# Seven block products instead of eight in the up projection of the last four feed-forward units

## The chip, the cores and the metric

One core of one Trainium2 chip. The metric is the device time of one execution, in microseconds, as the median of several runs. The profile of the kernel before is one execution taken by the hardware profiler; in it L416 means line 416 of the kernel before.

## The reference

Two layers with shared weights, each a long convolution over 2048 positions with 512 channels, and then a gated feed-forward network with 1792 features:

```python
def _A_ref(q, k, v, shift_k, ssm_k, ssm_D):
    ...                                   # k_shift: causal convolution of k with 4 taps
    kv = k_shift * v
    ...                                   # y: causal convolution of kv with ssm_k (length 2048), by FFT
    y = y + kv * ssm_D[None, None, :]
    return q * y

def _B_ref(x, w_gate, w_up, w_down):
    g = _silu(x @ w_gate)                 # x: 2048 x 512, w_gate and w_up: 512 x 1792
    u = x @ w_up
    return (g * u) @ w_down               # w_down: 1792 x 512

x = A_q
x = x + _A_ref(_layernorm(x, axis=-1), A_k, A_v, A_shift_k, A_ssm_k, A_ssm_D)
x = x + _B_ref(_layernorm(x, axis=-1), B_w_gate, B_w_up, B_w_down)
x = x + _A_ref(_layernorm(x, axis=-1), A_k, A_v, A_shift_k, A_ssm_k, A_ssm_D)
x = x + _B_ref(_layernorm(x, axis=-1), B_w_gate, B_w_up, B_w_down)
return x
```

All inputs and the output are bfloat16.

## The kernel before

The 2048 positions are cut into four blocks (c = 0 to 3) of 512. The convolution is computed once, as products of block spectra (tiles X, G, Z), because k, v and the filter are the same in both layers; its result for a block is the tile Yk. A **unit** (layer, c, h) is 256 positions of one layer: half h of block c. There are 16 units. The order of the program text is, for each c: (0,c,0), (0,c,1), (1,c,0), (1,c,1), with the convolution of later blocks between. So the last four units are (0,3,0), (0,3,1), (1,3,0), (1,3,1), and (1,3,0) needs the result of (0,3,0), as (1,3,1) needs that of (0,3,1).

**Before a unit** (`prologue`): mean and variance of the rows of x (L914, L915 on VectorE, the power -1/2 on GpSimd at L905), the normalised rows n, the product with Yk (L986) and the sum into x (L987), then the second norm, whose result z (L964) is transposed by a DMA that SyncE issues (L994) into zT: 128 channels by 4 channel blocks by 2 row sets by 128 rows.

**A unit** (`ffn`) goes through the 14 feature tiles of 128 features in groups of 4, 4, 4 and 2 (`GROUPS`). For a group there are two forms:

- *Column-wise* (from L1169): the weights are stationary and zT moves, so that features come out on the partitions and 256 positions in the columns. Matmuls of 256 columns write a PSUM tile pf (L416, the helper `mm`), two feature tiles in one bank. ScalarE copies gate values through Silu into sg (L1183) and up values into ht (L1187), and VectorE multiplies them (L1190).
- *Row-wise* (`by_rows`): zT is stationary and 512 weight columns move (also L416). ScalarE evacuates to sg and hr (L1123, L1124), VectorE multiplies (L1127, L1130), and a DMA transpose issued by SyncE (L1132) turns the product back into sg.

`ROWWISE` says how many of a unit's groups, from the first, take the row-wise form: 2 in (0,3,0), 1 in (0,3,1), 2 in (1,3,0), 0 in (1,3,1). For the down product of some groups (`STRASSEN`: all four groups in (0,3,0), (0,3,1) and (1,3,0), the first two in (1,3,1)) the kernel already uses seven block products instead of eight: sums of weight blocks made once by `weight_sums` (L1049), sums of activations cb (L1064, L1066, L1068 on VectorE), matmuls of 256 columns (L1085), four PSUM banks evacuated by ScalarE into mt (L1097) and combined into x by VectorE (L1102 to L1109). Other groups use the plain down product into pd (L1210).

**Order.** All operations are first put into a plan with the buffers that they read and write. Buffers are taken from rings of fixed size; "pf" has 4 PSUM banks, "s8" 11 slots of SBUF, "ht" 7. The table `ORDER` gives each operation of the plan its place in one overall sequence, and so fixes the order of instructions on each engine. It holds 1716 places.

Of the kernel before, what the change touches and what calls it, by code (L numbers as in the profile page):

```python
# [9 lines left out]
P = 128  # L10
F32 = mybir.dt.float32
# [3 lines left out]
ALU = mybir.AluOpType  # L15
# [13 lines left out]
ROWWISE = lambda l, c, h: 0 if (l, c, h) == (0, 0, 0) else {(0, 3, 0): 2, (0, 3, 1): 1, (1, 3, 0): 2, (1, 3, 1): 0}[l, c, h] if c == 3 else 3 if l == 1 else 2  # L29
ROWSPLIT = lambda l, c, h: 3 if c == 3 else 2  # L30
STRASSEN={(1,2,1):4,(0,3,0):4,(0,3,1):4,(1,3,0):4,(1,3,1):2}
I_RING = lambda k: "pf" if k == 3 else "pc"
# [311 lines left out]
def kernel(  # L344
# [175 lines left out]
    def dve(n, fn, r, w, one=False, cost=None, **kw):  # L520
        add("DVE", cost or (tt1(n) if one else tt2(n)), fn, r=r, w=w, **kw)
# [1007 lines left out]
```

## Time and profile before

| | |
|---|---|
| median of 3 runs | 339.26 us (339.04 to 339.29) |
| span of the profiled execution | 337.7 us (the page gives no other time of it) |
| instructions | 5898 |
| TensorE matmuls | 330.9 us busy, 2141 recorded |
| VectorE | 299.9 us busy |
| ScalarE | 262.8 us busy |
| GpSimd | 35.4 us busy |

The span runs from the first to the last instruction of that execution. Ends of matmuls are modelled, so the spacing of their starts says more than their durations. Groups of instructions are named by line, engine, operation, and the tiles written and read (out<-in); the number behind x counts them. A timeline row gives start, length, engine, line, operation, tiles, shape and count of a stretch of like instructions.

### The profile page before, as it was taken

How to read it: one execution, taken by the hardware profiler on the slowest of the kernel's cores; microseconds unless marked ns; L12 is line 12 of the kernel's file. 1: busy time of each engine (PE TensorE's matmuls, PEld its weight loads, DVE VectorE, ACT ScalarE, POOL GpSimd, SP SyncE). 2: the span in 40 equal slices, each digit the busy share in tenths (PEclk: the TensorE clock that was granted, in tenths of full speed). 3: DMA queues.
4: the chain of work that ended last, by engine and by line, in shares of the span. 5: the costliest groups of instructions: out<-in, count | busy, mean ns of one | idle time of the engine just before them, and what ended most of it. 6: DMA issues, size and time to landing. Idle time of an engine off the chain costs nothing.

```text
span 337.7 us, 5898 instructions
## 1 busy us (share of the span) xinstructions
PE 330.9 (98%) x2141; PEld 204.6 (61%) x2172; DVE 299.9 (89%) x512; ACT 262.8 (78%) x534; POOL 35.4 (10%) x48
## 2 busy tenths in 40 slices
PE   9999999999999999999999999999999999999996
PEld 7655864645445564745454464744455687858884
DVE  8899999999888998999999999999999787877545
ACT  7889999999967466999899894999675556475462
POOL 4050001102100000122010100011100100100000
PEclk9999999999999999999999999999999999999999
DMA  7999604632346147421324434510514230204101
GB/s 255 350 229 376 130 13 66 151 82 41 71 93 94 36 91 188 95 49 32 62 53 106 97 60 110 138 35 16 96 28 82 56 72 17 48 18 93 49 3 62
DMA packets 77993, 31.59 MB, mean 94 GB/s; under 512 B 69766, under 2 KB 75787, under 8 KB 77963
## 3 DMA queue, kind: packets, MB, share of 16 engines
q1 hardware_dynamic: 77808, 31.13, 39.6%
q8 instruction: 17, 0.28, 0.4%
q14 instruction: 14, 0.11, 0.1%
q10 hardware_dynamic: 154, 0.07, 0.1%
HBM read 12.33 MB, written 2.10 MB: 43 GB/s over the span
## 4 chain that ended last, share of the span: by engine, by line
PE 91%; ACT 4%; DMA 2%; issue 1%; DVE 1%; SPq 1%
PE pf L416 56%; PE pd L1210 20%; PE ps L1085 7%; PE ps L416 6%; DMA kTb<-in_A_k_dram 1%; PE wm L1495 1%; DMA sg<-hr 1%; ACT H L525 1%; SPq L1132 1%; ACT ks L620 1%; ACT n L959 0%; ACT jk L929 0%; DVE t L748 0%; ACT ev L525 0%; ACT hr L1124 0%
## 5 line engine op out<-in xcount | busy, mean ns | idle before, releaser
L416 PEld LDWEIGHTS <-zT 128*128 128x128 bf16 x528 | 51.6, 98 | 58.5 <-DMA zT<-z 0.2
L416 PE MATMUL pf<-wg_sb,zT 128*128 128x512 bf16 x255 | 64.3, 379 | 0.5
L416 PE MATMUL pf<-wu_sb,zT 128*128 128x512 bf16 x260 | 64.3, 379 | 0.2
L1210 PE MATMUL pd<-wd_sb,sg 128*128 128x512 bf16 x189 | 48.1, 379 | 0.9 <-DMA sg<-hr 0.3
L1124 ACT CAST hr<-pf 128x512 bf16<-128x512 f32 x66 | 38.4, 593 | 12.4 <-PE pf L416 8.5
L1123 ACT ACTIVATE sg<-pf 128x512 bf16<-128x512 f32 x66 | 38.8, 608 | 11.3 <-PE pf L416 10.2
L416 PE MATMUL pf<-zT,wg_sb 128*128 128x256 bf16 x368 | 46.0, 273 | 0.1
L416 PE MATMUL pf<-zT,wu_sb 128*128 128x256 bf16 x368 | 45.9, 273 | 0.0
L758 DVE TENSOR_TENSOR t<-X,G 128x4096 bf16<-128x4096 bf16 x18 | 40.9, 2284 | 0.1
L416 PEld LDWEIGHTS <-wu_sb 128*128 128x128 bf16 x368 | 36.0, 98 | 8.1
L416 PEld LDWEIGHTS <-wg_sb 128*128 128x128 bf16 x368 | 35.9, 98 | 7.9 <-issue 0.4
L1183 ACT ACTIVATE sg<-pf 128x512 bf16<-128x512 f32 x46 | 27.3, 607 | 10.8 <-PE pf L416 10.8
L1187 ACT CAST ht<-pf 128x512 bf16<-128x512 f32 x46 | 26.8, 595 | 9.8 <-PE pf L416 8.0
L905 POOL TENSOR_TENSOR rstd<-mv,nhalf 128x2 f32<-128x2 f32 x20 | 17.0, 852 | 158.2 <-DVE mv L915 134.7
L1210 PEld LDWEIGHTS <-sg 128*128 128x128 bf16 x200 | 19.5, 98 | 21.7 <-DMA sg<-hr 0.8
L1210 PE MATMUL pd<-wd_sb,ht 128*128 128x512 bf16 (+1 forms) x124 | 29.7, 369 | 0.1
L914 DVE BATCH_NORM_STATS2 bst<-xc 128x6 f32<-128x512 bf16 x40 | 26.5, 683 | 0.5
L905 POOL TENSOR_TENSOR rstd<-ve,nhalf 128x2 f32<-128x2 f32 x12 | 14.6, 1218 | 111.7 <-ACT ve L942 111.7
L1190 DVE TENSOR_TENSOR ht<-ht,sg 128x512 bf16<-128x512 bf16 (+1 forms) x31 | 16.6, 544 | 8.8 <-ACT sg L1183 4.5
L1130 DVE TENSOR_TENSOR hr<-hr,sg 128x1024 bf16<-128x1024 bf16 x27 | 18.4, 682 | 4.2 <-ACT sg L1123 2.0
L1210 PEld LDWEIGHTS <-ht 128*128 128x128 bf16 x126 | 12.3, 98 | 13.1 <-DVE ht L1190 0.3
L525 ACT ACTIVATE X<-ps 128x512 bf16<-128x512 f32 x32 | 18.4, 604 | 1.6 <-PE ps L416 0.9
(143 smaller groups left out, 522.1 us busy)
## 6 DMA issues: line engine op xcount, KB each, us to landing
hn<-in_A_ssm_k_dram SPq DMA_DIRECT2D x4, 512.0 KB, 3.7
vt<-in_A_v_dram SPq DMA_DIRECT2D x4, 512.0 KB, 5.5
xc<-in_A_q_dram SPq DMA_DIRECT2D x4, 512.0 KB, 5.6
out_dram<-xc SPq DMA_DIRECT2D x15, 128.0 KB, 1.9
wg_sb<-in_B_w_gate_dram SPq DMA_DIRECT2D x1, 1792.0 KB
wu_sb<-in_B_w_up_dram SPq DMA_DIRECT2D x1, 1792.0 KB, 8.9
wd_sb<-in_B_w_down_dram SPq DMA_DIRECT2D x1, 1280.0 KB, 12.1
sg<-hr SPq DMA_TRANSPOSE x66, 2.4
```

The costliest lines, as they stand in the source:

```text
L416: nc.tensor.matmul(o, lhsT=lhsT, rhs=rhs, start=(n == 0), stop=(n == len(terms) - 1))
L525: add("ACT", act(D), lambda: nc.scalar.activation(out=view(), in_=ps.t[:], func=ACT.Copy, scale=scale), r=[ps], w=[(buf, keys)], conv=conv)
L758: dve(8 * D, lambda t=t, part=part: nc.vector.tensor_mul(out=t.t[:], in0=x.t[:, :, part:part + 1, :].to_broadcast((P, R, 2, D)), in1=g.t[: ...
L905: add("POOL", cost, lambda: nc.gpsimd.tensor_tensor(out=rstd.t[:], in0=var(), in1=nhalf.t[:].to_broadcast((P, n)), op=ALU.pow), r=reads + ...
L914: add("DVE", 0.6, lambda st=st, i=i: nc.vector.bn_stats(out=st.t[:, 0:6], in_=xs[c].t[:, i, :]), r=[(xs[c], (i,))], w=[st])
L1085: nc.tensor.matmul(bank.t[:, half_ * C:(half_ + 1) * C], lhsT=lhsT(i), rhs=rhs(i), start=(first and i == 0 and half_ == 0), stop=(last and ...
L1123: add("ACT", act(D), lambda ps=ps, dst=dst, o=o, which=which: nc.scalar.activation(out=rows(dst, o), in_=ps.t[:], func=ACT.Silu) if which ...
L1124: out=rows(dst, o), in_=ps.t[:], func=ACT.Silu) if which == "g" else nc.scalar.copy(out=rows(dst, o), in_=ps.t[:]),
L1130: dve(n * W, lambda: nc.vector.tensor_mul(out=hr.t[:], in0=hr.t[:], in1=sg.t[:]), [sg], [hr], due=(unit, k / pairs, 0.0, "h"))
L1183: add("ACT", act(D), lambda ps=ps, o=o, sg=sg: nc.scalar.activation(out=sg.t[:, o:o + 2, :], in_=ps.t[:], func=ACT.Silu), r=[ps], w=[(sg, ...
L1187: add("ACT", act(D), lambda ps=ps, o=o, ht=ht: nc.scalar.copy(out=ht.t[:, o:o + 2, :], in_=ps.t[:]), r=[ps], w=[(ht, (o // 2,))], due=(uni ...
L1210: nc.tensor.matmul((pds[o] if not cs.start else pds[HP]).t[:, cs], lhsT=ht.tiles(q, o), rhs=wt["d"].t[:, ft, cs], start=(ft == std0 and no ...
```

## The change

In the second and third group (gi 1 and 2) of each of the last four units, the up product is computed by seven products of blocks instead of eight. A group's 512 features by 512 channels by 256 positions is cut in two along each of the three: feature tiles of even and odd number, the first and second pair of channel blocks, and the two row sets. Each of the seven products has 2 x 2 matmuls of 128 columns, 28 in all in place of 16 of 256. This takes:

- five sums of weight blocks for each of the two groups, made once (`up_sums`), five operations of 512 elements on VectorE each;
- sums of blocks of zT for each unit (`z_sums`), two operations of 512 and one of 256 on VectorE;
- four PSUM banks for a group's products instead of two, three full and one half full, which ScalarE copies into a tile of its own;
- four operations of 512 elements on VectorE for a group, which put the up values into ht.

The new tiles come from the ring "s8". The gate product of these groups stays, in the column-wise form. For that the second groups of (0,3,0) and (1,3,0), row-wise before, become column-wise: `ROWWISE` is 1 there. The plan has 1798 operations instead of 1716, and `ORDER` is a new table that differs from the start on. A helper makes the view of a statistics buffer at its first use.

```diff
-ROWWISE = lambda l, c, h: 0 if (l, c, h) == (0, 0, 0) else {(0, 3, 0): 2, (0, 3, 1): 1, (1, 3, 0): 2, (1, 3, 1): 0}[l, c, h] if c == 3 else 3 if l == 1 else 2
+ROWWISE = lambda l, c, h: 0 if (l, c, h) == (0, 0, 0) else {(0, 3, 0): 1, (0, 3, 1): 1, (1, 3, 0): 1, (1, 3, 1): 0}[l, c, h] if c == 3 else 3 if l == 1 else 2
+UP7 = {(0,3,0): (1, 2), (0,3,1): (1, 2), (1,3,0): (1, 2), (1,3,1): (1, 2)}
 ORDER = [
-    7, 79, 141, 188, 2, 3, 1, 15, 23, 4, 12, 0, 5, 13, 68, 9, 10, 6, 8, 11, 28, 19, 14, 24, 20, 25, 32, 33, 38, 69, 144, 146, 18, 46, 17, 45, 22, 43,
...
+    8, 81, 208, 209, 3, 1, 0, 5, 17, 4, 7, 10, 11, 12, 36, 14, 9, 15, 2, 16, 18, 20, 21, 19, 24, 27, 29, 30, 32, 45, 53, 54, 33, 34, 13, 37, 35,
...
+    def up_sums(gi, kw):
+
+        fts = range(sum(GROUPS[:gi]), sum(GROUPS[:gi + 1]))
+        m = len(fts) // 2
+        t = wsum[gi] = new("s8", "wu", [P, 5, KD // 2, m, P], parts=5)
+        part = lambda k, f: wt["u"].t[:].rearrange("p k (t f) -> p k t f", f=P)[:, 2 * k:2 * k + 2, fts[0] + f:fts[-1] + 1:2]
+        for n, (a, b, op) in enumerate((((0, 0), (1, 1), ALU.add), ((0, 1), (1, 1), ALU.add), ((0, 0), (1, 0), ALU.add),
+                                        ((0, 1), (0, 0), ALU.subtract), ((1, 0), (1, 1), ALU.subtract))):
+            dve(2 * m * P, lambda n=n, a=a, b=b, op=op: nc.vector.tensor_tensor(out=t.t[:, n], in0=part(*a), in1=part(*b), op=op),
+                [wt["u"]], [(t, (n,))], **kw)
+
+    def z_sums(unit, zT, kw):
...
+        dve(KD * P, lambda: nc.vector.tensor_add(out=strided(t.t[:], K2 * P, [[P, KD], [1, P]]), in0=at(0, [[W, KD]]), in1=at(P, [[W, KD]])),
+            [zT], [(t, (1,))], **kw)
+        dve(KD * P, lambda: nc.vector.tensor_sub(out=t.t[:, 3:5], in0=at(P, [[K2 * W - P, 2], [W, K2]]),
+                                                 in1=at(K2 * W + P, [[-K2 * W - P, 2], [W, K2]])), [zT], [(t, (2,))], **kw)
+        dve(K2 * P, lambda: nc.vector.tensor_add(out=t.t[:, 0], in0=at(0, [[W, K2]]), in1=at(K2 * W + P, [[W, K2]])), [zT], [(t, (0,))], **kw)
+
+    def up_seven(unit, zT, ht, fts, gi, at):
...
+        for n, (rd, terms) in enumerate((
+                ([wt["u"], (z7, (2,))], ((lambda i: raw(0, 0, i), both(3)), (lambda i: raw(1, 1, i), both(4)))),
+                ([w7, zT], ((lambda i: summed(2, i), tok(1, 1)), (lambda i: summed(1, i), tok(0, 0)))),
+                ([w7, (z7, (1,))], ((lambda i: summed(4, i), both(2)), (lambda i: summed(3, i), both(1)))),
+                ([(w7, (0,)), (z7, (0,))], ((lambda i: summed(0, i), both(0)),)))):
+            ps = new("pf", "pf", [P, 2, m, P], F32)
+
+            def go(ps=ps, terms=terms):
+                todo = [(h_, i, kk, lhsT, rhs) for h_, (lhsT, rhs) in enumerate(terms) for i in range(m) for kk in range(K2)]
+                for q, (h_, i, kk, lhsT, rhs) in enumerate(todo):
+                    nc.tensor.matmul(ps.t[:, h_, i], lhsT=lhsT(i)(kk), rhs=rhs(kk), start=(q == 0), stop=(q == len(todo) - 1))
+            add("PE", pe(len(terms) * m * K2, P), go, r=rd, w=[ps], due=(unit, at, 0.0, None))
+            add("ACT", act(len(terms) * m * P), lambda n=n, ps=ps, terms=terms: nc.scalar.copy(out=mt.t[:, n, 0:len(terms)], in_=ps.t[:, 0:len(terms)]),
+                r=[ps], w=[(mt, (n,))], due=(unit, at, 1.5, "a"))
...
+        dve(2 * m * P, lambda: nc.vector.tensor_add(out=strided(ht.t[:], tk, [[tile - tk, 2], [2 * tile, m], [1, P]]), in0=mt.t[:, 1],
+                                                    in1=mt.t[:, 0]), [(mt, (0, 1))], [(ht, keys)], **kw)
+        dve(2 * m * P, lambda: nc.vector.tensor_sub(out=mt.t[:, 2], in0=mt.t[:, 2], in1=mt.t[:, 1]), [(mt, (1,))], [(mt, (2,))], **kw)
+        dve(2 * m * P, lambda: nc.vector.tensor_add(out=mt.t[:, 2], in0=mt.t[:, 2], in1=mt.t[:, 3:4, 0].to_broadcast((P, 2, m, P))),
+            [(mt, (3,))], [(mt, (2,))], **kw)
+        dve(2 * m * P, lambda: nc.vector.tensor_add(out=strided(ht.t[:], 0, [[tile + tk, 2], [2 * tile, m], [1, P]]), in0=mt.t[:, 2],
+                                                    in1=strided(mt.t[:], m * P, [[-m * P, 2], [P, m], [1, P]])), [(mt, (0, 2))], [(ht, keys)], **kw)
...
+                seven_up = gi in UP7.get(unit, ())
                 for o in range(0, n, 2):
-                    for which in ("g", "u"):
+                    for which in ("g",) if seven_up else ("g", "u"):
...
+                if seven_up:
+                    up_seven(unit, zT, ht, fts, gi, k / pairs)
                 dve(n * W, lambda sg=sg, ht=ht: nc.vector.tensor_mul(out=ht.t[:], in0=ht.t[:], in1=sg.t[:]), [sg], [ht],
```

More of the change, by code (lines that the diff above doesn't have):

```diff
@@ L907, in power, with stat_slot @@
         return rstd
+    def stat_slot(slot):
+        if bst.t is None:
+            bst.t = bst.make(0)
+        return bst.t[:, slot]
     def ln_stats(c, rows, pw=PW):
@@ L912, in ln_stats @@
         for o, i in enumerate(rows):
-            st = plan.buf("bn", "bnst", lambda slot: bst.t[:, slot])
+            st = plan.buf("bn", "bnst", stat_slot)
             add("DVE", 0.6, lambda st=st, i=i: nc.vector.bn_stats(out=st.t[:, 0:6], in_=xs[c].t[:, i, :]), r=[(xs[c], (i,))], w=[st])
@@ L1109, in add_seven @@
         dve(D, lambda: nc.vector.tensor_add(out=ends(), in0=ends(), in1=two(2)), [(mt, (2,))], [(x, rows)], **kw)
+    wsum, zsum = {}, {}
+    def up_sums(gi, kw):
[7 more added lines that the diff above has]
+                [wt["u"]], [(t, (n,))], **kw)
@@ new lines, in z_sums @@
+    def z_sums(unit, zT, kw):
+        t = zsum[unit] = new("s8", "zs", [P, 5, KD // 2, P], parts=3)
+        at = lambda off, dims: strided(zT.t[:], off, dims + [[1, P]])
+        K2 = KD // 2
+        dve(KD * P, lambda: nc.vector.tensor_add(out=strided(t.t[:], K2 * P, [[P, KD], [1, P]]), in0=at(0, [[W, KD]]), in1=at(P, [[W, KD]])),
[3 more added lines that the diff above has]
+        dve(K2 * P, lambda: nc.vector.tensor_add(out=t.t[:, 0], in0=at(0, [[W, K2]]), in1=at(K2 * W + P, [[W, K2]])), [zT], [(t, (0,))], **kw)
@@ new lines, in up_seven @@
+    def up_seven(unit, zT, ht, fts, gi, at):
+        m, K2 = len(fts) // 2, KD // 2
+        kw = dict(due=(unit, at, 0.0, "h"))
+        if gi not in wsum:
+            up_sums(gi, kw)
+        if unit not in zsum:
+            z_sums(unit, zT, kw)
+        w7, z7 = wsum[gi], zsum[unit]
+        mt = new("s8", "m7", [P, 4, 2, m, P], parts=4)
+        raw = lambda k, f, i: (lambda kk: wt["u"].t[:, k * K2 + kk, (fts[0] + 2 * i + f) * P:(fts[0] + 2 * i + f + 1) * P])
+        summed = lambda n, i: (lambda kk: w7.t[:, n, kk, i])
+        tok = lambda k, o: (lambda kk: zT.t[:, k * K2 + kk, o, :])
+        both = lambda n: (lambda kk: z7.t[:, n, kk])
+        for n, (rd, terms) in enumerate((
[11 more added lines that the diff above has]
+                r=[ps], w=[(mt, (n,))], due=(unit, at, 1.5, "a"))
+        tile, tk = ht.steps
+        keys = range(m)
+        dve(2 * m * P, lambda: nc.vector.tensor_add(out=strided(ht.t[:], tk, [[tile - tk, 2], [2 * tile, m], [1, P]]), in0=mt.t[:, 1],
[5 more added lines that the diff above has]
+                                                    in1=strided(mt.t[:], m * P, [[-m * P, 2], [P, m], [1, P]])), [(mt, (0, 2))], [(ht, keys)], **kw)
```

132 rows, old and new, of the table ORDER are left out of this document.

## The prediction

> **What bounds the kernel now.** I read the page first, then who waited for whom on TensorE, then the busy time by stage, then the timelines of TensorE, VectorE and the SyncE queue over the last four units.
>
> ```profile
> span 337.7 us, 5898 instructions
> PE 330.9 (98%) x2141; PEld 204.6 (61%) x2172; DVE 299.9 (89%) x512; ACT 262.8 (78%) x534; POOL 35.4 (10%) x48
> ...
> DVE  8899999999888998999999999999999787877545
> ...
> PEclk9999999999999999999999999999999999999999
> ...
> PE 91%; ACT 4%; DMA 2%; issue 1%; DVE 1%; SPq 1%
> ```
>
> TensorE is busy for 98% of the span and makes up 91% of the chain that ended last; its clock is granted in full throughout. The busy row alone could mislead, since ends of matmuls are modelled, so I ask what TensorE ever waited for:
>
> ```profile
> engine line waited for: us in total, times, longest us
> PE ps L416 <- DMA kTb<-in_A_k_dram: 0.8, 1, 0.8
> PE wm L1495 <- PEq L1513: 0.8, 1, 0.8
> PE pd L1210 <- DMA sg<-hr: 0.3, 1, 0.3
> PE ps L416 <- ACT ks L620: 0.2, 1, 0.2
> ```
>
> That is the whole list: 2.1 us in four waits, none of them in the last four units. So the time is the sum of matmul spacings plus a short head and tail. Every matmul nanosecond removed is worth a nanosecond, as long as no other engine makes TensorE wait. VectorE is the next one, at 89%; by stage:
>
> ```profile
> core 0: us, PE busy (x) PEld busy (x) DVE busy (x) ACT busy (x) POOL busy (x), PEclk, DMA share, GB/s
> 240.00:260.00 20.00, 19.52 (x104) 10.12 (x105) 19.07 (x31) 12.78 (x23) 0.71 (x1) 1.00 0.31 62
> 260.00:270.00 10.00, 10.00 (x62) 5.91 (x61) 7.85 (x19) 5.14 (x10) 1.57 (x1) 1.00 0.31 53
> 270.00:280.00 10.00, 9.95 (x89) 8.56 (x88) 7.46 (x20) 6.13 (x12) 0.00 (x0) 1.00 0.32 64
> 280.00:290.00 10.00, 10.00 (x81) 7.79 (x80) 8.56 (x20) 6.14 (x12) 1.83 (x2) 1.00 0.18 41
> 290.00:300.00 10.00, 9.95 (x78) 7.53 (x78) 8.48 (x25) 4.74 (x10) 0.00 (x0) 1.00 0.14 29
> 300.00:310.00 10.00, 10.00 (x77) 7.35 (x76) 6.78 (x18) 7.34 (x13) 1.39 (x2) 1.00 0.26 52
> 310.00:320.00 10.00, 10.00 (x95) 8.95 (x93) 5.82 (x18) 4.76 (x9) 0.00 (x0) 1.00 0.26 67
> 320.00:330.00 10.00, 10.00 (x94) 8.96 (x92) 5.09 (x14) 6.96 (x14) 0.00 (x0) 1.00 0.01 2
> ```
>
> VectorE's idle time is 0.9 us in 240 to 260, then 2.15, 2.54, 1.44, 1.52, 3.22, 4.18 and 4.91: 20.0 us in 260 to 330, of which 10.9 lie before 310. The four units of the change run there. This is the room for what the change adds.
>
> **TensorE: removed and added.** The spacing of matmuls by width, from starts in the timeline:
>
> ```profile
> 28.45 1.06 PE L416 MATMUL ps<-dg,kTb 128*128 128x128 bf16 x16
> 29.35 0.81 PE L895 MATMUL ps<-m,inv 128*128 128x512 bf16 x3
> ...
> 262.10 1.89 PE L416 MATMUL pf<-wg_sb,zT 128*128 128x512 bf16 x8
> 263.82 1.89 PE L416 MATMUL pf<-wu_sb,zT 128*128 128x512 bf16 x8
> ...
> 287.00 3.66 PE L416 MATMUL pf<-zT,wu_sb 128*128 128x256 bf16 x32
> 290.49 0.38 PE L1085 MATMUL ps<-wsa,sg 128*128 128x256 bf16 x2
> ```
>
> So 0.90 / 16 = 0.056 us for 128 columns, 1.72 / 8 = 0.215 for 512, 3.49 / 32 = 0.109 for 256. Eight groups (two in each of four units) change their up product. Six are column-wise already: 16 matmuls of 256 columns, 1.745 us, become 28 of 128 columns, 1.575. That is 0.17 each, 1.02 in all. The other two (second group of (0,3,0) and of (1,3,0)) were row-wise: gate and up together 16 of 512, 3.44 us; after, gate 16 of 256 and up 28 of 128, 3.32. That is 0.12 each, 0.24 in all. Sum: **1.26 us less on TensorE**, all of it on the path.
>
> The 28 short matmuls each load their own weights. The 16 quoted above do too (128x128 taps against 128 columns), so 0.056 is the nearest row. The Trainium skill speaks against it: "TensorE: Matmul & The Clock Gate", section "Back-to-back issue gap", gives about 81 ns per matmul for a sustained stream of 128-column pairs and calls 56 ns the isolated gap. By that figure the up product of a group would take an estimated 2.27 us, and the change would cost about 4.3 us instead of saving 1.26. This trace disagrees: its 16-long run keeps 0.056. I take 0.056, and keep the other as a rival, priced below from rows.
>
> **VectorE: added.** Each operation on 512 bf16 elements, and on 256, by starts:
>
> ```profile
> 274.62 0.42 DVE L1066 TENSOR_TENSOR cb<-sg 128x512 bf16<-128x512 bf16 x1
> 274.96 0.42 DVE L1066 TENSOR_TENSOR cb<-ht 128x512 bf16<-128x512 bf16 x1
> ...
> 293.30 0.28 DVE L1068 TENSOR_TENSOR cb<-sg 128x256 bf16<-128x256 bf16 x1
> 293.50 0.28 DVE L1068 TENSOR_TENSOR cb<-ht 128x256 bf16<-128x256 bf16 x1
> ```
>
> 0.34 us and 0.20 us. These too are strided sums of 128-wide blocks, as the new ones are. Weight sums: 2 groups x 5 x 0.34 = 3.4 us, once. Sums of zT: 4 units x (2 x 0.34 + 0.20) = 3.5. Recombination: 8 groups x 4 x 0.34 = 10.9. Together 17.8 us, beside 20.0 of idle time in 260 to 330. Per unit it is 3.6 us. Before 310 fall the weight sums and two units, 3.4 + 7.2 = 10.6 against 10.9 idle; after 310 two units, 7.2 against 9.1. It fits, with almost nothing to spare in the first part. The pieces are small (0.34) and the idle time comes in waits for ScalarE and GpSimd that such pieces can fill, so I cost it at a little rather than at nothing: 0.3 us of new TensorE waits. The ends are 0, if all pieces fit, and 3.2 (second rival).
>
> **ScalarE, PSUM, queues.** Evacuations, and the issues that feed the units:
>
> ```profile
> L1187 ACT CAST ht<-pf 128x512 bf16<-128x512 f32 x19 | 10.7, 586 | 5.0 <-PE pf L416 3.4 <-PE pd L1210 1.2 <-DVE ht L1190 0.3
> ...
> L1097 ACT CAST mt<-ps 128x512 bf16<-128x512 f32 x15 | 8.7, 591 | 8.3 <-PE ps L1085 8.2
> ...
> L1097 ACT CAST mt<-ps 128x256 bf16<-128x256 f32 x5 | 1.9, 384 | 0.2 <-PE ps L1085 0.2
> ```
>
> A group's two up copies (2 x 0.586 = 1.17) become three of 512 and one of 256 (2.16): 0.98 more, 7.9 over eight groups. ScalarE is busy 41.2 of the 70 us in 260 to 330, so 28.8 are free. A product fills a bank in 8 x 0.056 = 0.45 us where a copy takes 0.59; four "pf" banks take that up if other matmuls stand between, and the gate and down products are there to stand between. Cost: zero; without that cover 0.14 us a bank. On the SyncE queue four transposes (sg<-hr) go with the two row-wise groups, and so does their landing time; nothing waited for them in these units, so no gain. The tail after the last matmul is made by group 4 and the output, which stay. Sum: 1.26 - 0.3 = about 1.0 us less of the 337.7 span. The page gives no time of that execution but its span, which lies 1.56 us (0.46%) under the median of 339.26; I take that remainder as fixed. **Forecast 338.2 us.** A measurement of this kernel can tell 0.2%, 0.7 us, from no change.
>
> **Rivals.** *First: the new order, not the blocks, decides.* The table that fixes every engine's order differs from its first entries on, so the waits at the head are drawn again: the 0.8 for the transposed load of the keys (kTb), 0.3 and 0.2. If they went, another 1.3 us would go with them: 336.9. If the new order makes as much again somewhere else, the saving is eaten: 339.3. The present order left TensorE only these waits in 337 us, which speaks for small numbers on both sides.
>
> *Second, slower: VectorE holds up the start of (1,3,1).*
>
> ```profile
> 309.01 2.52 SPq L994 DMA_TRANSPOSE zT<-z x2
> ...
> 313.55 1.91 PE L416 MATMUL pf<-zT,wg_sb 128*128 128x256 bf16 x16
> ...
> zT<-z SPq DMA_TRANSPOSE x10, 2.4
> ```
>
> The two transposes of (1,3,1) are issued from 309.01 in 2.52, the second at about 310.3, and land 2.4 later at 312.7; their first reader starts at 313.55. The margin is 0.9 us. TensorE will get there earlier by three units' saving, 1.26 x 3/4 = 0.9, so the margin is gone before VectorE is asked anything. In the stretch from the end of (0,3,1) to here VectorE must do that unit's sums and norms, and now 3.6 us more for (1,3,0), beside 3.2 idle us in 300 to 310. Any of it that stands ahead of the norms' steps delays the landing one for one. From 1.3 us the saving is gone; if most of it does, 3.2, the time is 339.26 - 1.26 + 3.2 = 341.2. For it: the margin. Against it: the (1,3,0) pieces are wanted by the down product of (1,3,0), which can be put after other work, and idle time elsewhere (9.1 after 310) lets them wait. The same place one unit earlier has more room:
>
> ```profile
> 290.60 5.27 SPq L994 DMA_TRANSPOSE zT<-z x2
> ...
> 296.71 1.03 PE L416 MATMUL pf<-wg_sb,zT 128*128 128x512 bf16 x3
> ```
>
> There the first transpose lands at 293.0, 3.7 us ahead of its reader.
>
> *Third: short matmuls are bound by their weight loads.*
>
> ```profile
> L416 PEld LDWEIGHTS <-wu_sb 128*128 128x128 bf16 x368 | 36.0, 98 | 8.1
> ```
>
> A load lasts 98 ns. If loads did not overlap, 28 would take 2.74 us: 1.0 more than now in each of eight groups, 8 us, 347.3 in all. Against it: the quoted run of 16 at 56 ns has the same loads. The skill's 81 ns is a weaker form of the same.
>
> **Chances.** Forecast, saving of 0.7 to 1.5 arriving: 0.50. First rival's gain, beyond 1.5: 0.06. Saving eaten to within 0.7 either way by waits of either rival: 0.16. Second rival, slower by over 0.7: 0.26. Third: 0.02. So faster 0.56, same 0.16, slower 0.28. The likeliest case alone is 337.7 to 338.6. The range for 8 in 10 reaches to most of the first rival's gain below, 337.1, and to the full price of the second above, 341.2.
>
> **What would show it.** Right: the up product's matmuls spaced by 0.056; TensorE's waits in the last four units under 0.5 us; VectorE's idle time from 260 on down to a few us; the last matmul about 1 us earlier. Wrong: a wait of TensorE for zT or for a VectorE result (ht, cb, zs) in the last 80 us; 128-column matmuls at 0.08 or more; or the waits of the first 33 us grown, which would make the order the cause and not the blocks.

## The result, and the profile after

The kernel became slower: 342.31 us (median of 15 runs, 340.31 to 343.87) against 339.47 for the kernel before in the same comparison (15 runs, 339.04 to 339.96). The ratio is 1.0078, with a 95% interval of 1.0066 to 1.0090. The forecast was 338.2, in a range of 337.1 to 341.2. The profiled execution of the kernel after took 342.96 us, 0.65 above the median, so the profiles differ by more than the medians. One execution in the experiments, of 351.98 us at a mean granted clock of 0.956, was in a slower state of the chip and is in none of the times below.

The page of the kernel after, its lines that answer to those of before:

```profile
span 341.1 us, 6215 instructions
PE 331.3 (97%) x2269; PEld 208.7 (61%) x2300; DVE 315.7 (93%) x566; ACT 271.1 (79%) x550; POOL 39.3 (12%) x48
PE 89%; DMA 5%; SPq 3%; ACT 1%; DVE 1%; issue 1%
```

The span is 3.4 us longer, and the chain that ended last now holds 5% of DMA where it held 2%. That is a sign of a wait for data. Who waited for whom on TensorE in the kernel after:

```profile
engine line waited for: us in total, times, longest us
PE ptz L1034 <- DVE z L976: 2.5, 1, 2.5
PE wm L1572 <- PEq L1590: 0.8, 1, 0.8
PE ps L423 <- DMA kTb<-in_A_k_dram: 0.6, 1, 0.6
PE ps L423 <- DVE vt L628: 0.4, 1, 0.4
PE pt L479 <- DMA kn<-in_A_k_dram: 0.2, 1, 0.2
```

One wait is new and large: 2.5 us for z of the first unit, at 31 us, where before z cost TensorE nothing that this view lists. None of the five lies in the last four units, where the blocks are. There the busy time by stage says that VectorE took its added work:

```profile
core 0: us, PE busy (x) PEld busy (x) DVE busy (x) ACT busy (x) POOL busy (x), PEclk, DMA share, GB/s
290.00:300.00 10.00, 9.95 (x96) 8.64 (x95) 9.82 (x30) 5.67 (x11) 0.70 (x1) 1.00 0.23 41
...
260.00:330.00 70.00, 69.77 (x692) 58.30 (x694) 62.27 (x174) 48.17 (x95) 4.24 (x6) 1.00 0.21 42
```

VectorE was busy 50.0 us in 260 to 330 before and is 62.3 now; its idle time fell from 20.0 to 7.7 us, in 290 to 300 to 0.2, and TensorE stayed full. The seven-block products are these (timeline of TensorE):

```profile
286.58 0.61 PE L1171 MATMUL pf<-zT,wu 128*128 128x128 bf16 x8
287.03 0.83 PE L1171 MATMUL pf<-zs,wu 128*128 128x128 bf16 x12
287.70 0.61 PE L1171 MATMUL pf<-zs,wu_sb 128*128 128x128 bf16 x8
288.14 0.61 PE L1171 MATMUL pf<-zs,wu 128*128 128x128 bf16 x8
```

From 286.58 to 288.14 run 28 matmuls of 128 columns: 0.0557 us each. With the spacings of the trace (0.0558, 0.1092 and 0.2158) a group saves 0.185 us, and a row-wise one 0.144: 6 x 0.185 + 2 x 0.144 = 1.40 us.

So where did the time go? The chain in order of time, from 20 us, in the kernel after:

```profile
20.45 12.25 DMA xc<-in_A_q_dram
32.70 0.02 issue
32.72 0.69 DVE bst L926
33.42 0.32 DVE z L976
33.74 0.05 issue
33.79 0.72 PE ptz L1034 x8
```

The load is the x of block 1, which nobody needs yet. The new order puts VectorE's first statistics over that x (bst, L926) ahead of the z of the first unit. On VectorE z comes next after them, so z, whose inputs were there (the last, rstd of GpSimd, at 30.92), stands behind a load of 12 us, and TensorE's transposes of z stand behind z (timeline of TensorE):

```profile
33.79 0.72 PE L1034 MATMUL ptz<-ident,z 128*128 128x128 bf16 x8 [2.55 <-DVE z L976]
```

In the kernel before the same z ran at 31.08, and the first statistics of block 1 at 38.71 (timeline of VectorE, before):

```profile
31.08 0.73 DVE L964 TENSOR_SCALAR z<-xc,mv,rstd 128x512 bf16<-128x512 bf16 x2 [0.25 <-POOL rstd L905]
...
38.71 0.69 DVE L914 BATCH_NORM_STATS2 bst<-xc 128x6 f32<-128x512 bf16 x1
```

The idle time is not the whole loss (slices of 1 us, kernel after; the column behind POOL's is the clock that TensorE was granted):

```profile
34.00:35.00 1.00, 1.00 (x16) 0.74 (x14) 1.00 (x4) 0.99 (x3) 0.00 (x0) 1.00 1.71 45
35.00:36.00 1.00, 1.00 (x14) 0.94 (x12) 1.00 (x2) 1.00 (x4) 0.00 (x0) 0.64 0.88 201
36.00:37.00 1.00, 1.00 (x6) 0.75 (x5) 1.00 (x2) 1.00 (x4) 0.00 (x0) 0.50 1.39 128
37.00:38.00 1.00, 1.00 (x7) 0.69 (x6) 0.96 (x2) 0.78 (x3) 0.00 (x0) 0.50 0.42 92
38.00:39.00 1.00, 1.00 (x8) 0.77 (x7) 1.00 (x3) 1.00 (x4) 0.00 (x0) 0.66 0.00 0
```

TensorE is busy again, at the full clock, from 33.79, and then the granted clock falls to a half until 38.7. The shortfall is 0.36 + 0.50 + 0.50 + 0.34 = 1.7 us. A matmul of 256 columns is spaced by 0.213 there and by 0.109 after it.

The end changed too (timeline of before, then of after: TensorE's last products, and the two final adds on VectorE):

```profile
333.19 1.47 PE L1210 MATMUL pd<-wd_sb,ht 128*128 128x256 bf16 x12
333.28 0.69 DVE L1217 TENSOR_TENSOR xc<-xc,pd 128x512 bf16<-128x512 bf16 x1
334.48 0.42 DVE L1226 TENSOR_TENSOR xc<-xc,pd 128x256 bf16<-128x256 bf16 x1 [0.51 <-PE pd L1210]
```

```profile
335.65 1.91 PE L1287 MATMUL pd<-wd_sb,ht 128*128 128x256 bf16 x14
336.94 0.42 DVE L1303 TENSOR_TENSOR xc<-xc,pd 128x256 bf16<-128x256 bf16 x1 [0.90 <-PE pd L1287]
337.37 0.69 DVE L1294 TENSOR_TENSOR xc<-xc,pd 128x512 bf16<-128x512 bf16 x1
```

TensorE's work ends at 334.66 before and at 337.56 after. From there to the end are 3.04 and 3.54 us: the tail grew by 0.50, with the larger add and its output now last. From the start of the last matmul, as the expectations count it, that is 3.31 and 3.81. The rest of the 3.4 us is the last matmul, later by 2.89 us. Adding up how far each matmul's spacing exceeds the usual one for its width, I get some 4.1 us of waits and half clock before and 8.3 after. The difference, 4.2, less the saving of 1.40 makes 2.8, which fits the 2.89.

### The profile page after: what moved, and what is told of

Same layout as the page of the kernel before. It is cut to its first block, busy times and chain, and to the rows that moved or that the text cites. A ratio compares the mean times of both kernels' runs of the same rounds, so it can differ in the third digit from the quotient of the medians.

```text
span 341.1 us, 6215 instructions
## 1 busy us (share of the span) xinstructions
PE 331.3 (97%) x2269; PEld 208.7 (61%) x2300; DVE 315.7 (93%) x566; ACT 271.1 (79%) x550; POOL 39.3 (12%) x48
## 2 busy tenths in 40 slices
DMA packets 75817, 31.08 MB, mean 91 GB/s; under 512 B 67589, under 2 KB 73610, under 8 KB 75786
## 4 chain that ended last, share of the span: by engine, by line
PE 89%; DMA 5%; SPq 3%; ACT 1%; DVE 1%; issue 1%
PE pf L423 53%; PE pd L1287 20%; PE ps L1097 7%; PE ps L423 4%; PE pf L1171 4%; DMA xc<-in_A_q_dram 4%; SPq L1459 2%; DMA kn<-in_A_k_dram 1%; SPq L467 1%; ACT ev L532 0%; ACT kTb L485 0%; PE ptz L1034 0%; DVE G L560 0%; DVE bst L926 0%; DVE xc L1294 0%
## 5 line engine op out<-in xcount | busy, mean ns | idle before, releaser
L423 PEld LDWEIGHTS <-zT 128*128 128x128 bf16 x496 | 48.3, 98 | 54.6 <-DMA zT<-z 0.6
L423 PE MATMUL pf<-wu_sb,zT 128*128 128x512 bf16 x243 | 60.6, 379 | 0.4
L423 PE MATMUL pf<-wg_sb,zT 128*128 128x512 bf16 x237 | 60.3, 379 | 0.4
L423 PE MATMUL pf<-zT,wg_sb 128*128 128x256 bf16 x400 | 51.1, 276 | 0.1
L423 PEld LDWEIGHTS <-wg_sb 128*128 128x128 bf16 x400 | 39.3, 99 | 8.3
L423 PE MATMUL pf<-zT,wu_sb 128*128 128x256 bf16 x272 | 35.0, 276 | 0.0
L423 PEld LDWEIGHTS <-wu_sb 128*128 128x128 bf16 x272 | 26.9, 99 | 6.5
L926 DVE BATCH_NORM_STATS2 bst<-xc 128x6 f32<-128x512 bf16 x40 | 26.6, 683 | 2.5 <-DMA xc<-in_A_q_dram 2.0
L1262 ACT CAST ht<-pf 128x512 bf16<-128x512 f32 x34 | 20.1, 610 | 6.7 <-PE pf L423 6.6
L1267 DVE TENSOR_TENSOR ht<-ht,sg 128x1024 bf16<-128x1024 bf16 (+1 forms) x33 | 18.0, 556 | 2.0 <-ACT sg L1258 1.7
L1173 ACT CAST m<-pf 128x512 bf16<-128x512 f32 (+1 forms) x32 | 16.2, 546 | 3.2 <-PE pf L1171 3.1
```

The lines of the kernel that those rows point to most:

```text
L423: nc.tensor.matmul(o, lhsT=lhsT, rhs=rhs, start=(n == 0), stop=(n == len(terms) - 1))
L926: add("DVE", 0.6, lambda st=st, i=i: nc.vector.bn_stats(out=st.t[:, 0:6], in_=xs[c].t[:, i, :]), r=[(xs[c], (i,))], w=[st])
L1262: add("ACT", act(D), lambda ps=ps, o=o, ht=ht: nc.scalar.copy(out=ht.t[:, o:o + 2, :], in_=ps.t[:]), r=[ps], w=[(ht, (o // 2,))], due=(uni ...
L1267: dve(n * W, lambda sg=sg, ht=ht: nc.vector.tensor_mul(out=ht.t[:], in0=ht.t[:], in1=sg.t[:]), [sg], [ht], due=(unit, k / pairs, 0.0, "h"))
```

## Experiments

Theory A: the blocks save what was costed, and the order of the head loses it. Rivals: the blocks' own work on VectorE costs the time, or the wait for z has another cause. In the diffs, `moved(table, ops, behind)` is an added helper that puts operations, by number, behind another one in the overall order. 518 and 520 are VectorE's first statistics of block 1, 498 is ScalarE's first sum over the same x, 287 is the load.

**Statistics of block 1 later, on both engines.**

```diff
+ORDER = moved(moved(ORDER, [518, 520], 246), [498], 205)
```

> The changed kernel with three steps moved later in its order: the two statistics on VectorE and the first sum on ScalarE that read the x of block 1, which in the changed kernel stand ahead of the first unit's z and of the copy of its zT and wait there for a load. Blocks and the rest of the order unchanged. Theory A (the loss is this place in the order: 2.55 us of waiting for z, and the clock that drops behind it): the wait for z falls from 2.55 to at most 0.6 us, the clock is granted in full again, the time falls from 342.3 to 338.0 to 338.7 us. Theory B (the loss is in the last units: VectorE's extra work or the short matmuls): the time stays at 341 or above.

Measured: 339.49 us (339.20 to 340.16), ratio to the kernel before 0.9999 (0.9990 to 1.0008). Three operations in other places win back 2.8 us; no block product was touched, and the mean clock is 0.998 to 1.000 in every execution. The waits of TensorE in its profile, the first four rows:

```profile
PE wm L1586 <- PEq L1604: 0.8, 1, 0.8
PE ps L437 <- DVE vt L642: 0.5, 1, 0.5
PE pt L493 <- DMA kn<-in_A_k_dram: 0.4, 1, 0.4
PE ptz L1048 <- DVE z L990: 0.2, 1, 0.2
```

The wait for z fell from 2.5 to 0.2. Theory A's mechanism held, but its time, 338.0 to 338.7, was missed by 0.8 us: something else keeps the rest of the saving back, and the last two parts of this section look for it.

**On VectorE alone.**

```diff
+ORDER = moved(ORDER, [518, 520], 222)
```

> As the first, but only the two statistics on VectorE are moved (behind the copy of zT); ScalarE's sum over the same x stays ahead of its own copy of zT. Theory A: z is in time (wait for it under 0.6 us), but ScalarE now makes the first gate product wait about 1 to 1.5 us for zT; 339.3 to 341 us. Theory B: 341 or above.

Measured: 340.50 us (339.92 to 342.08), ratio 1.0036 (1.0018 to 1.0055). VectorE's statistics carry most of it. ScalarE's sum, left where it was, keeps a part: `PE ps L437 <- ACT X L546` with 0.7 us is among the waits. X is copied right behind that sum; the expectation had named zT, the copy after it.

**The same fault in the kernel before, without any block product.**

```diff
+ORDER = moved(ORDER, [518], 261)
```

> The kernel before, without any block product, with one step moved: the first statistics over the x of block 1 put ahead of the first unit's z on VectorE, as in the changed kernel. Theory A: VectorE then waits for that load, which in the kernel before lands at about 34.4 us (issued at 21.6, 12.8 to landing) where z started at 31.1; TensorE waits about 3 us for z and the clock drops behind it; 342 to 345 us. Theory B: 339.2 to 339.8, no change.

Measured: 343.37 us (3 runs, 343.10 to 343.40), ratio 1.0108 (1.0093 to 1.0124). One VectorE operation in another place costs the kernel before 3.8 us. Its profile shows the same wait and, in the slices behind it, the same half clock:

```profile
PE ptz L1036 <- DVE z L978: 1.9, 1, 1.9
...
36.00:38.00 2.00, 2.00 (x11) 1.40 (x10) 1.97 (x4) 1.46 (x4) 0.00 (x0) 0.50 0.46 105
```

**The wait filled with matmuls**, to part the idle time from the clock. Forty matmuls of 128 columns into an unused part of a bank stand ahead of the transposes of z.

```diff
             if o in fill:
                 warm(*fill[o])
+            if o.n == 221:
+                warm("pf", place[o.bufs[-1]], 40)
```

> The changed kernel with 40 dummy matmuls of 128 columns on TensorE just ahead of the transposes that wait for z, so that TensorE is not idle there; their result is not used. Theory A1 (the halved spacing from 34.7 to 39 us follows from TensorE being idle for 2.5 us): the wait stays, the clock is granted in full, 340.3 to 341.0 us in all runs. Theory A2 (the clock drop has another cause): 342 to 342.6, clock at 0.995 as before.

Measured: 343.83 us (343.17 to 345.92), ratio 1.0135 (1.0106 to 1.0163): slower than the kernel after. The part about the clock is confirmed; the time expected with it, 340.3 to 341.0, was missed. The forty matmuls end where the wait ended (the transposes of z start at 33.37), and behind them the clock stays whole:

```profile
36.00:38.00 2.00, 2.00 (x21) 1.79 (x19) 1.97 (x3) 2.00 (x6) 0.00 (x0) 1.00 0.20 44
```

The time rose all the same: new waits ate what the clock gave back (waits of TensorE, then the DMA answer for 240 to 246 us):

```profile
PE pf L425 <- DMA zT<-z: 1.2, 2, 0.9
PE pd L1289 <- DMA sg<-hr: 0.8, 1, 0.8
```

```profile
q8 instruction: 1, 0.02, 1.6%
...
sg<-hr SPq DMA_TRANSPOSE x2, 4.1
```

The queue that loads instructions moves one packet in that stretch, of 0.02 MB, and the two transposes beside it land after 4.1 us where the page gives 2.5 for all of them. Another such packet lies in 50 to 58 us, where zT's transposes take 3.4. Forty matmuls and their weight loads are 80 instructions more on TensorE, so each later packet comes at another point of the work: these two lie at 53.0 and 241.3 us here, and at 63.4 and 249.6 in the kernel after. There the transposes of 50 to 58 us and the two sg<-hr issued from 241 on took 2.4 to 2.6 us. So the slow transposes moved with the packets. Over the sixteen kept traces the transposes sg<-hr that had a packet of instructions under way took 3.25 us in the median (194 of them), those that had none 2.45 (546, of which ten took more than 3.0). No run moved a packet and nothing else, so this is a strong link, not a proof.

**The load ahead of the weights**, with the kernel's own order otherwise: block 1's x goes out before the up and down weights.

```diff
+ORDER = moved(ORDER, [287], 78)
...
-        load_x(c, after=[wd])
+        load_x(c, after=[k1])
```

> The changed kernel with its own order, but the load of block 1's x is issued on the SyncE queue ahead of the loads of the up and down weights instead of behind them. Theory A (VectorE waits at the statistics for this load): it lands before VectorE comes to it, the wait for z falls from 2.55 us to under 0.6, the clock stays full, 338.5 to 339.8 us, unless the up weights, now later, make the first up product wait, which the waits would name. If the place of the statistics has nothing to do with it: 341.5 to 342.5.

Measured: 339.33 us (338.79 to 339.94), ratio 0.9992 (0.9983 to 1.0002), 3.0 us under the kernel after. The statistics stand where they stood; only what they wait for comes sooner (SyncE's queue, kernel after and this version):

```profile
20.45 4.15 SPq L499 DMA_DIRECT2D xc<-in_A_q_dram  x1
```

```profile
18.60 0.58 SPq L513 DMA_DIRECT2D xc<-in_A_q_dram  x1
```

With the runs before it this settles the large loss from both sides: move what waits, or move what it waits for.

**A new order for the head.** The seven-block products stay; the first 352 or so places follow the order of the kernel before, though not place by place. Places 650 to 1500 are those of the kernel after, and what lies between and the last 250 were ordered again, with a longer time allowed for the load. So more than the head differs.

```diff
-        return add("SP", 0.7, lambda: nc.sync.dma_start(out=xs[c].t[:], in_=q_t[:, c]), w=[xs[c]], lat=(7.5, 10.5, 5.0, 4.0)[c], due=due, after=after)
+        return add("SP", 0.7, lambda: nc.sync.dma_start(out=xs[c].t[:], in_=q_t[:, c]), w=[xs[c]], lat=(7.5, 13.3, 5.0, 4.0)[c], due=due, after=after)
```

> The changed kernel with all its block products, its order replaced in the first 50 us by that of the kernel before (and then smoothed step by step, there and in the last few us) so that no statistics over the x of block 1 stand ahead of the first unit's z. The order from there to the last unit stays that of the changed kernel. Theory A (the blocks save their 1.39 us, 56 ns by 28 matmuls; the head's order lost it): head waits as in the kernel before, the last matmul about 1.0 to 1.4 us earlier than in the kernel before, 338.2 to 338.9 us. Theory B (with the blocks in, some other part pays for them): 339.3 us or more.

Measured: 339.21 us (339.03 to 339.92), ratio 0.9994 (0.9985 to 1.0003). The wait for z went, the head's other waits shrank, and the last matmul starts at 333.52, 0.87 us earlier than before. The rest of the 1.4 us was lost in waits new between 60 and 110 us (1.4 us of spacing; the longest single wait there is 0.5 us, for zT), and in the tail.

**More work on VectorE in the new units**, to find where the second rival begins: in the version just shown each of the four recombination steps of a group is done with one more addition of 512 elements; and once the first step alone.

```diff
+        more = lambda: nc.vector.tensor_add(out=mt.t[:, 4], in0=mt.t[:, 1], in1=mt.t[:, 1])
...
-        dve(2 * m * P, lambda: nc.vector.tensor_sub(out=mt.t[:, 2], in0=mt.t[:, 2], in1=mt.t[:, 1]), [(mt, (1,))], [(mt, (2,))], **kw)
+        dve(2 * m * P, lambda: (nc.vector.tensor_sub(out=mt.t[:, 2], in0=mt.t[:, 2], in1=mt.t[:, 1]), more()), [(mt, (1,))], [(mt, (2,))], **kw)
```

> The first kernel of this set with each of the four recombination steps on VectorE followed by one more of the same size whose result is not used: 32 x 0.34 = 10.9 us more on VectorE in the last four units. VectorE had 7.7 us of idle time left in 260 to 330 in the changed kernel. If it is close to being the bound: at least 3 us slower than the first kernel of this set, with TensorE waiting for VectorE's results in the last four units. If it has room to spare by moving into other gaps: under 1 us slower.

> As the second, but only the first recombination step of each group is followed by an extra one: 8 x 0.34 = 2.7 us more on VectorE. If VectorE's load does not yet decide, as the absence of waits in the last 80 us says: within 0.5 us of the first kernel of this set. If it does (the prediction's second rival): 1 us or more slower.

Measured: with all four steps 345.29 us (ratio 1.0172, 1.0154 to 1.0190), 6.1 us more than the version without; with the first alone 340.29 us (ratio 1.0019, 1.0010 to 1.0028), 1.1 us more. In the first, VectorE's results hold up TensorE in the last units:

```profile
PE ps L1094 <- DVE cb L1073: 2.8, 4, 0.8
```

So a form of the second rival's mechanism is real: of 11 us of added work 6.1 come through, and by the spacing of matmuls 5.9 of them lie behind 260 us. For 2.7 us of added work the times differ by 1.1, just over the 1 us that was to speak for the rival. The profile of that run carries it in part only: behind 260 us TensorE lost 0.5 us more than without the added work, ahead of products of cb; another 0.4 is a longer wait for zT at 107 us, where nothing was added. How near the work of the change itself lies to the edge is therefore not measured closely.

**What keeps the mended version from the forecast.** The version with the load first still waits 0.5 us for vt and 0.4 for z in the head, and it has one wait in the new units: `PE ps L1111 <- DVE cb L1090: 0.4, 1, 0.4`, at 260.6 us. VectorE's steps before that cb had themselves waited 1.1 us for a transpose (sg<-hr). Neither trial touches that one. First trial: sixteen matmuls that need neither go ahead of the one over vt.

```diff
 ORDER = moved(ORDER, [287], 78)
+ORDER = moved(ORDER, [262], 256)
```

> The version with the load of block 1 issued early (339.33 us), with one more TensorE operation moved: sixteen 128-column matmuls of 0.9 us, which need neither vt nor z, go ahead of the first matmul over vt instead of behind the z transposes. There TensorE waited 0.50 us for vt and then 0.43 us for z. Theory A (what is left of the gap to the forecast lies in such waits and in the tail, each worth its own length on TensorE): the vt wait goes, VectorE writes z by the same time as before, and of the z wait some of the 0.43 us goes too; 338.4 to 338.9 us. Rival B (the time of this kernel has a floor elsewhere, and each wait that is taken away comes back later): within 0.2 us of 339.3.

Measured: 339.36 us (338.93 to 339.95), ratio 0.9996 (0.9987 to 1.0005). Rival B: the waits came back one step later.

```profile
PE pf L438 <- ACT zT L1054: 0.6, 1, 0.6
```

Second trial: the statistics that stand ahead of the copies of zT go behind them as well.

```diff
+ORDER = moved(moved(moved(ORDER, [518, 520], 246), [498], 205), [224], 219)
```

> The version with the early load and the covered vt wait (339.36 us), with the four statistics that stand ahead of the two copies of zT on their engines moved behind them (on VectorE the two over block 1's x; on ScalarE the first sum over block 1's x and the sum over block 0's x). In that version the wait of TensorE had come back as 0.62 us (0.80 of spacing) at the first gate product, for zT. Theory A (the head is a chain from x through VectorE and ScalarE to zT, 0.3 to 0.6 us longer than in the kernel before because these statistics stand in it; TensorE work moved into it only moves the wait): the wait for zT falls under 0.3 us and the time by 0.3 to 0.6 us, 338.7 to 339.1. Rival B (the zT chain is set by something else, such as the reciprocal root on GpSimd that z needs): wait and time within 0.2 us of the version before, 339.2 to 339.5.

Measured: 340.26 us (339.53 to 340.69), ratio 1.0017 (1.0007 to 1.0026), slower than without. Theory A fell, and the time lies above rival B's 339.2 to 339.5 too. The wait for zT only shrank to 0.5 us, and the statistics, now later on ScalarE, hold up the copies that free the gate's banks:

```profile
PE pf L439 <- ACT sg L1274: 0.9, 2, 0.6
```

**The tail.** Moving only the last matmuls of 512 columns, their add and their output, in the version with the cover:

```diff
+ORDER = moved(moved(moved(ORDER, [1789], 1783), [1792], 1789), [1793], 1792)
```

> The version before it in this call, with the tail in the order of the kernel before: the last 512-column down products, their final add on VectorE and their 128 KB output stand ahead of the last 256-column ones. Theory A (the changed tail costs 0.4 to 0.5 us after the last matmul: 3.8 us from its start to the end where the kernel before had 3.3): 0.3 to 0.5 us less than the version before it, 338.0 to 338.5 us, and under the kernel before by 1.0 to 1.5 us. Rival B (the end is set by the last matmul and the fixed closing alone, the order of the last outputs being worth nothing): within 0.15 us of the version before it.

Measured: 339.29 us (338.94 to 339.74), ratio 0.9993 (0.9984 to 1.0001); from the start of the last matmul to the end 3.84 us. Nothing was gained, since the add still waited for its matmul until 333.54. So the product that feeds it had to move too: last up product (1786), its cast and its product with the gate, then the rest.

```diff
+ORDER = moved(moved(ORDER, [1786, 1787], 1703), [1788], 1707)
+ORDER = moved(ORDER, [1789, 1792, 1793], 1711)
```

> The version before it in this call, with the last up product, its cast and its product with the gate moved ahead of two of the last groups of seven, so that the 512-column down products end before the 256-column ones begin, as in the kernel before (where the 512-element add ran 1.2 us ahead of the last add; moving only the add, in a version shown already, left it waiting for its matmul until 1.1 us later, and 3.84 us from the last matmul to the end). Theory A (the tail costs 0.4 to 0.5 us): from the start of the last matmul to the end 3.3 to 3.4 us instead of 3.8, and the time 0.3 to 0.5 us under the version before it, 338.2 to 338.8. Rival B (the three last outputs, not the order of their adds, set the tail): 3.7 to 3.9 us and the same time within 0.15 us.

> The version with the load of block 1 issued early and nothing else (339.33 us), with the tail as in the last version shown: last up product, its cast and product earlier, the 512-column down products and their output ahead of the 256-column ones. Theory A (of the 1.39 us that the blocks save, about 0.7 us is left in the head and 0.4 to 0.5 us in the tail): the time from the start of the last matmul to the end falls from 3.82 to 3.3 to 3.5 us, and the time by 0.3 to 0.5 us, to 338.8 to 339.1, which is under the kernel before by about 0.15%. Rival B (the earlier last output only moves the end's wait elsewhere): within 0.15 us of 339.3, and no difference from the kernel before.

> The same tail in the version that also has the sixteen 128-column matmuls ahead of the first one over vt (339.36 us without this tail). Theory A: 338.8 to 339.1, as the one before it in this call, since its head waits are as long in sum (2.1 against 2.0 us between 20 and 60 us). Rival B: 339.2 to 339.5.

Measured, in the same order: 339.87 us (ratio 1.0006, 0.9997 to 1.0015), 0.39 under the version without this tail; 338.95 us (338.57 to 339.96, ratio 0.9988, 0.9978 to 0.9997), 0.38 under it; 338.91 us (338.27 to 342.57, ratio 0.9990, 0.9971 to 1.0010), 0.45 under it. The last two are compared with versions of other comparisons, in which the kernel before stood within 0.03 us. Three times the same size, so theory A holds here: the tail costs some 0.4 us. From the start of the last matmul to the end are now 3.50, 3.49 and 3.45 us, where 3.76, 3.82 and 3.86 stood without this tail. The final adds, in the second of these versions:

```profile
333.02 0.68 DVE L1310 TENSOR_TENSOR xc<-xc,pd 128x512 bf16<-128x512 bf16 x1
...
334.10 0.42 DVE L1319 TENSOR_TENSOR xc<-xc,pd 128x256 bf16<-128x256 bf16 x1 [0.40 <-PE pd L1303]
```

The large add runs 1.1 us ahead of the small one again. With the load first and this tail the seven-block kernel stands 0.57 us under the kernel before. Its interval just excludes no change; that of the version with the cover and the same tail does not, so this gain is at the edge of what these runs can tell.

## Why the prediction was wrong, point by point

- **TensorE, 1.26 us less.** Right; it is 1.40, by the finer spacings. 128 columns stand at 0.0558 us over all such gaps in the seven-block products.
- **VectorE, 17.8 us more beside 20.0 idle, at 0.3 us of new waits.** Right in what matters: 15.8 us more busy in all by the page, 12.2 of it in 260 to 330, and no wait of TensorE in the last 80 us is listed (the spacings show 0.2 us there, ahead of a product of cb at 263.9). That there was not much to spare was right too: 11 us more cost 6.1.
- **ScalarE, 7.9 us more at no cost.** Right: 8.3 by the page, and no wait.
- **Second rival** (VectorE holds up (1,3,1)). It did not happen, though the time it gave, 341.2, lies nearer the result than the forecast. A slower time is no proof of its mechanism; the waits tell.
- **Third rival** (short matmuls bound by weight loads). Refuted by 0.0557 us over 28 in a row. The Trainium skill, "TensorE: Matmul & The Clock Gate", section "Back-to-back issue gap", has about 81 ns for such a stream; by it the change would have cost an estimated 4.3 us, and this trace shows a saving of 1.40 in the matmuls.
- **First rival: the step that failed.** "If the new order makes as much again somewhere else, the saving is eaten: 339.3" priced what a new order can lose by what the old one lost, 1.3 us, and "The present order left TensorE only these waits in 337 us, which speaks for small numbers on both sides" took the old order's quality for a property of the work. The term measured 4.2 us (2.6 of idle, 1.7 of half clock, small waits both ways). The prediction's last part named the sign to look for, grown waits in the first 33 us, and that is what showed. The diff could have priced it: a table new "from its first entries on" leaves open what stands ahead of z, and the load of 12 us and the clock's answer to idle time had no term.
- **"The tail ... which stay."** Wrong by 0.5 us. What is computed at the end stayed; its order did not.
- **The rest.** Without the fault in the head (339.33 us) the kernel stands 0.2 us under the one before, where TensorE's 1.4 would have put it 1.4 under. Of the difference 0.4 is the tail, shown by three pairs of runs. That leaves about 0.8 us. By the spacings of its profile TensorE loses 0.4 us more in the head than before, behind vt and z, and 0.5 ahead of cb at 260.6; the wait for sg<-hr at 240 us, 0.5 in the kernel before, is gone. The first 16 us are 0.5 longer, but they differ by 0.4 between executions of three versions with the same head. The head's waits came back in other forms in two trials and were not got rid of, so the cause of these 0.8 us stays open.

## What to carry to other kernels

Where an edit comes with a new order, price the order by itself: on each engine, look for the first instruction that waits for a load, and ask what stands behind it and who waits for that. A wait of TensorE can cost more than its length: behind those of 2.5 and 1.9 us here the granted clock fell to a half for 3.4 us. And a saving in matmuls is kept only if the last add and the last output still come early.

## What the runs showed of the hardware

- **The clock falls after the wait, not in it.** TensorE stood still from 31.24 to 33.79 us, worked at the full clock until 35.3, and then at half until 38.7. The kernel before with the moved statistics did the same after a wait of 1.9 us. The clock's record in the two traces is full from 4.55, half from 35.27 and full again from 38.68 us in the one, and 4.46, 35.18 and 38.59 in the other: both times 30.72 us and then 3.41, nine to one. Of the last 3.41 us before the fall TensorE was idle for 1.9 in both. The Trainium skill, "TensorE: Matmul & The Clock Gate", section "Part 1: The HAM clock gate (the "warmup" mystery)", describes a free-running window of 3.4 us that sets the clock, and asks for an idle window of that length before it drops. The lengths of 30.72 and 3.41 us agree with the window; a fall after one that was idle for 1.9 us does not agree with a whole idle one. That the window runs free would explain why the same kernel may escape: three of its fifteen executions have a mean clock of 0.999 or 1.000 and took 340.31, 340.32 and 341.64 us, the other twelve, at 0.995 or 0.990, 341.53 to 343.87. A version without the long wait is not quite safe from it: one of twelve executions with the cover and the tail, where the profile lists no wait over 0.8 us, has 0.995 too and took 342.57.
- **Loads of instructions go with slow DMA transposes**: 3.4 and 4.1 us to landing beside such a packet where all of a kind have 2.5 in the median, and 3.25 against 2.45 over all traces. So even instructions that run in idle time can move a wait to another place.
